# First loads, casts and V products of a fused attention and FFN kernel in another order

## The chip, the cores and the metric

The kernel runs on one core of a Trainium2 chip. The metric is the device time of one execution in microseconds. The kernel before took 264.7 us (median of three runs, 263.91 to 265.38).

## The reference

Attention over 4 batches, 8 heads, 768 positions and a head dimension of 64: every query sees the first 8 keys (the global ones) and the 96 keys up to its own position, with a bias that grows with the distance, differently in each head. The result, as 3072 tokens of 512 values, goes through a gated FFN. The inputs are float32 and so is the output.

```python
def _attn_ref(q, k, v, n_global, n_local):
    scores = scale * np.matmul(q, k.transpose(0, 1, 3, 2))
    is_global = pos[None, :] < int(n_global)
    is_local = (rel >= 0) & (rel < int(n_local))
    keep = is_global | is_local
    dist = np.where(is_global & ~is_local, float(n_local), np.abs(rel))
    scores = scores - slopes[:, None, None] * dist[None, :, :]
    scores = np.where(keep, scores, -1000000000.0)
    a = np.exp(scores - np.max(scores, axis=-1, keepdims=True))
    a = a / (np.sum(a, axis=-1, keepdims=True) + 1e-09)
    return np.matmul(a, v).astype(np.float32)

def _moe_ref(x, w_gate, w_val, w_out):
    gate = np.maximum(x @ w_gate, 0.0)
    val = x @ w_val
    return (gate * val @ w_out).astype(np.float32)
```

## The kernel before

The tokens are cut into eight halves of 384 queries (two for each batch). Each half goes through attention, head pair by head pair (four pairs of two heads), and the result `xT` (features by tokens) through the FFN: `gate` and `val` for twelve blocks of 128 hidden features, then `outp`. The order of everything is written out by hand: each engine executes its instructions in the order in which the program's calls issue them (a manual schedule), and engines wait for each other through semaphores that follow from the tiles. From the second half on, the attention of a later half is woven between the matmuls of an FFN; all FFN matmuls run on TensorE, which then hardly pauses. The change is in the first half (half 0 of batch 0), ahead of the first FFN matmul.

What the first half needs, and the names:

- `kq0`: its keys and queries in float32. `load_first(h0, h1)` issues two transfers on SyncE's queue, keys and then queries of heads h0 to h1 (line 180). Heads 0 to 1, 2 to 3, and 4 to 7 are loaded by three calls. The third is made later in the program: two one-element memsets on VectorE (line 551) write into the places that its transfers fill, so that these wait for VectorE to get there.
- `v3`: V of the first half, cast to bfloat16 by the transfer, on GpSimd's queue (line 207). Behind it on that queue: the first group of gate and value weights (`load_w_group(0)`, line 153), the keys and queries of the second half (`kq1`, four transfers, line 561), further V rows (`load_v`, line 136).
- `first_cast(p, i, copy)` (line 280): the keys (i = 0) or queries (i = 1) of head pair p to bfloat16, on VectorE (`V`), ScalarE (`A`) or GpSimd (`P`).
- `first_keys(p, copy_q)`: three transposes of the keys and three of the queries on TensorE (line 271), the queries copied to `qT` by the engine given (line 288), the keys by VectorE in three copies to `kT` (lines 258 to 260). `clear_keys(p)`: two memsets on VectorE ahead of that.
- `first_scores(0, p, g)`: bias (line 318, pairs 0 and 1 only) and score matmuls (line 327), then the exponential on ScalarE (line 333), for two groups g. `first_masks` multiplies by the bias mask on VectorE for pairs 2 and 3 (line 345); `make_mask(h)` builds a mask on ScalarE (line 238).
- `make_sel(n)` (line 235): one of three selection matrices, on VectorE. `first_values(j, copy)`: three matmuls with these bring the rows of `v3` into the order of the keys (line 303, here called the V products), and one copy by VectorE or ScalarE puts them into `vbuf` (line 305). `spread_v_globals(0, 4, NT)`: three small transfers on SyncE's queue that copy the global rows of V to later tiles (line 132).
- `first_av(0, p)`: denominators and numerators of a pair (line 448). `first_norm(0, p)`: Ln and Exp on ScalarE (lines 458 and 460) and the product `xT` on VectorE (line 463).

PSUM is given out in turn from two pools here: four tiles `t_ps` and two tiles `s_ps`.

Of the kernel before, what the change touches and what calls it, by code (L numbers as in the profile page):

```python
# [15 lines left out]
def kernel(  # L16
# [12 lines left out]
    nc = tc.nc  # L29

    B, H, S, D = q.shape
# [8 lines left out]
    NN = 3  # L40
# [4 lines left out]
    NT = -(-S // KT)  # L45
# [46 lines left out]
    vbuf = [const.tile([128, NT, (2 * H + 1) * D], BF16, name=f"vbuf{i}") for i in range(2)]  # L92
# [29 lines left out]
    def v_dst(b, r0, r1, j):  # L122
        t = vbuf[b % 2][r0:r1, j, D:]
        return t.rearrange("p (h z) -> p h z", z=2 * D)[:, :, 0:D]
# [5 lines left out]
    def spread_v_globals(b, j0=1, j1=NT):  # L130
        for j in range(j0, j1):
            nc.sync.dma_start(out=v_dst(b, 0, NG, j), in_=v_dst(b, 0, NG, 0))
# [22 lines left out]
    def load_w_group(i):  # L155
        load_w(wg[i], moe_w_gate, i * GW * 128, (i + 1) * GW * 128)
        load_w(wv[i], moe_w_val, i * GW * 128, (i + 1) * GW * 128)
# [13 lines left out]
    kq0 = firstp.tile([128, 2, H, NN * D], FP32, name="kq0")  # L171
# [6 lines left out]
    def load_first(h0, h1):  # L178
        for i, src in enumerate((k, q)):
            nc.sync.dma_start(out=kq0[:, i, h0:h1, :], in_=rows_of(src, 0, h0, h1))  # L180

    load_first(0, 2)
    load_first(2, 4)
    nc.scalar.preload_act_table_set("natural_log_exp_and_others")

    zeros = firstp.tile([128, 512], BF16)
# [43 lines left out]
    def clear_keys(p):  # L230
        nc.vector.memset(kT[0][p][:, 3, 32:128].bitcast(mybir.dt.uint32), 0)
        nc.vector.memset(kT[0][p][:, 6, NG + 48 : 128].bitcast(mybir.dt.uint32), 0)

    def make_sel(n):
        nc.vector.tensor_scalar(sel[:, n], sidx, float(n), None, op0=ALU.is_equal)
# [41 lines left out]
    def first_cast(p, i, copy):  # L277
        if p not in cast_of:
            cast_of[p] = cast_pool.tile([128, 2, NN, 2, D], BF16, name="qk")
        copy(cast_of[p][:, i].rearrange("t n e d -> t e n d"),  # L280
             kq0[:, i, 2 * p : 2 * p + 2, :].rearrange("t e (n d) -> t e n d", n=NN))

    def first_keys(p, copy_q):
        tp = psum["t"].tile([128, 512], FP32, name="t_ps")
        tp = tp[:, 0:QH].bitcast(BF16).rearrange("d (i t) -> d i t", i=2)
        for i in range(2):
            transposes(tp[:, i], cast_of[p][:, i], cast_n)
        copy_q(qTb[0][:, p, 0, :], tp[:, 1])
        put_keys(nc.vector.tensor_copy, nc.vector.tensor_copy, kT[0][p], tp[:, 0], 0)
# [10 lines left out]
    def first_values(j, copy):  # L300
        vt = psum["t"].tile([128, 512], FP32, name="t_ps")
        for n in range(NN):
            nc.tensor.matmul(vt, lhsT=sel[:, n, j, :], rhs=v3[:, :, n * D : (n + 1) * D],
                             start=(n == 0), stop=(n == NN - 1))
        copy(v_dst(0, 0, 128, j), vt.rearrange("r (h d) -> r h d", d=D))

    def first_scores(s, p, g):
        half = s % 2
        spans_ = [by[half, j] for j in steps_of[half][g]]
        ps = psum["s"].tile([128, 2, 512], FP32, name="s_ps")  # L310
        es = ef_pool.tile([128, 2, 360], BF16, name=f"ef{g}")
        cols = sum(NN * w for _, _, w, _ in spans_)
        qd = qTb[s][:, p, 0, :].rearrange("d (n t) -> d n t", n=NN)
        biased = p < HP // 2
        for e in range(2) if biased else ():
            c = 0
            for i, (j, a, w, m) in enumerate(spans_):
                nc.tensor.matmul(ps[:, e, c : c + NN * w].rearrange("k (n t) -> k n t", n=NN),
                                 lhsT=diag[:, 2 * p + e],
                                 rhs=dd[:, 0 if j == 0 else 1, :, m : m + w],  # L320
                                 start=(i == 0), stop=False, skip_group_check=True)
                c += NN * w
        c = 0
        for i, (j, a, w, m) in enumerate(spans_):
            for e in range(2):
                r = slice(64 * e, 64 * e + 64)
                nc.tensor.matmul(ps[:, e, c : c + NN * w].rearrange("k (n t) -> k n t", n=NN),  # L327
                                 lhsT=kT[0][p][r, j, :], rhs=qd[r, :, a : a + w],
                                 start=(i == 0 and not biased), stop=(i == len(spans_) - 1),
                                 skip_group_check=True)  # L330
            es_of[s, p, j] = (es, c)
            c += NN * w
        nc.scalar.activation(es[:, :, 0:cols], ps[:, :, 0:cols], AF.Exp, bias=0.0, scale=scale)  # L333

    def first_masks(s, p, g):
        for j in steps_of[s % 2][g]:
            _, a, w, m = by[s % 2, j]
            es, c = es_of[s, p, j]
            for_all = es[:, :, c : c + NN * w]
            mk = m_all[:, 2 * p : 2 * p + 2, 0 if j == 0 else 1, :, m : m + w]  # L340
            if w == WQ:
                mk = mk.rearrange("k e n p -> k e (n p)")
            else:
                for_all = for_all.rearrange("k e (n p) -> k e n p", n=NN)
            nc.vector.tensor_mul(for_all, for_all, mk)
# [92 lines left out]
    def first_av(s, p, of="t"):  # L438
        half = s % 2
        todo = [by[half, j] for g in steps_of[half] for j in g]  # L440
        av = [psum[of].tile([128, 512], FP32, name=f"{of}_ps") for _ in range(2)]
        for what in range(2):
            av3 = av[what][:, 0:QH].rearrange("d (n p) -> d n p", n=NN)
            for i, (j, a, w, m) in enumerate(todo):
                es, c = es_of[s, p, j]
                for e in range(2):
                    z0 = D + 2 * D * (2 * p + e)
                    nc.tensor.matmul(av3[64 * e : 64 * e + 64, :, a : a + w],  # L448
                                     lhsT=ones if what == 0 else vbuf[0][:, j, z0 : z0 + D],
                                     rhs=es[:, e, c : c + NN * w].rearrange("k (n p) -> k n p", n=NN),  # L450
                                     start=(i == 0), stop=(i == len(todo) - 1),
                                     skip_group_check=True)
        av_of[s, p] = av

    def first_norm(s, p):
        av = av_of[s, p]
        ln = rc_pool.tile([128, QH], FP32, name="lnd")
        nc.scalar.activation(ln, av[0][:, 0:QH], AF.Ln, bias=0.0, scale=1.0)  # L458
        rc = rc_pool.tile([128, QH], FP32, name="rcp")
        nc.scalar.activation(rc, ln, AF.Exp, bias=0.0, scale=-1.0)  # L460
        if s not in xT_of:
            xT_of[s] = xt_pool.tile([128, N_DC, QH], BF16, name="xT")
        nc.vector.tensor_tensor(xT_of[s][:, p, :], av[1][:, 0:QH], rc, op=ALU.mult)  # L463
# [77 lines left out]
    V, A, P = nc.vector.tensor_copy, nc.scalar.copy, nc.gpsimd.tensor_copy  # L541
# [5 lines left out]
    clear_keys(0)  # L547
    first_cast(0, 0, V)
    first_cast(0, 1, V)
    for i in range(2):  # L550
        nc.vector.memset(kq0[0:1, i, 4, 0:1], 0.0)
    load_first(4, H)
    first_cast(1, 0, V)
    first_cast(1, 1, A)
    first_keys(0, A)
    clear_keys(1)
    first_keys(1, A)
    load_w_group(0)
    for h0 in (0, 4):
        for i, src in enumerate((k, q)):  # L560
            nc.gpsimd.dma_start(out=kq1[:, i, h0 : h0 + 4, :], in_=rows_of(src, 1, h0, h0 + 4))
        if h0 == 0:
            first_cast(2, 0, P)
            first_cast(2, 1, P)
            first_cast(3, 0, P)
            first_cast(3, 1, P)
            nc.gpsimd.memset(vbuf[0][:, NT - 1, :].bitcast(mybir.dt.uint32), 0)
    for j in range(4, NT):
        load_v(0, j)
    first_scores(0, 0, 0)  # L570
    for n in range(NN):
        make_sel(n)
    first_scores(0, 0, 1)
    make_mask(5)
    first_scores(0, 1, 0)
    first_scores(0, 1, 1)
    first_values(0, V)
    first_values(1, A)
    first_values(2, V)
    first_values(3, A)  # L580
    spread_v_globals(0, 4, NT)
    clear_keys(2)
    first_keys(2, V)
    clear_keys(3)
    first_av(0, 0)
    first_keys(3, V)
    make_mask(6)
    first_scores(0, 2, 0)
    first_masks(0, 2, 0)
    first_scores(0, 2, 1)  # L590
    first_masks(0, 2, 1)
    first_norm(0, 0)
    first_av(0, 1)
    make_mask(7)
    first_scores(0, 3, 0)
    first_masks(0, 3, 0)
    first_scores(0, 3, 1)
    first_masks(0, 3, 1)
    first_norm(0, 1)
    first_av(0, 2)  # L600
    first_norm(0, 2)
# [101 lines left out]
```

## Time and profile before

| | |
|---|---|
| median of the runs | 264.7 us (263.91 to 265.38) |
| the profiled execution | 265.34 us |
| its span | 263.6 us |
| TensorE (PE) busy | 245.9 us, 93% |
| ScalarE (ACT) busy | 156.3 us, 59% |
| VectorE (DVE) busy | 130.7 us, 50% |
| GpSimd (POOL) busy | 91.8 us, 35% |
| first matmul of the FFN | 26.88 us |
| mean clock granted to TensorE | 0.973 |

The profile is of one execution on the hardware. Times are microseconds from the start of the span; durations of single instructions are often given in ns. PE is TensorE's matmul side and PEld its weight loads, SP is SyncE, and an engine's name with a q is its queue of instructions or transfers. A row of the timeline gives start, duration, engine, line, operation, the tiles (out<-in), a count, and in brackets the idle time before and what ended it. In a table of windows each row gives the stretch, the busy time of each engine in it with the number of its instructions, then the granted clock of TensorE (1.00 is full speed), the share of the DMA engines' time and GB/s. The chain that ended last is followed back from the last instruction, at each step to what released it.

### The profile page before, as it was taken

What the parts mean: (1) busy time and instruction counts of PE and PEld (TensorE: products, weight loads), DVE (VectorE), ACT (ScalarE), POOL (GpSimd) and SP (SyncE); (2) the same over time, 40 slices, a digit from 0 to 9 for tenths busy, and PEclk for the clock granted to TensorE, in tenths of its full rate; (3) what the DMA queues carried; (4) which work ended last, traced back from release to release, by engine and by line L of the source; (5) the groups of instructions that cost most, each with busy time, mean ns of one, the idle gap of its engine ahead of it and who ended that gap; (6) DMA issues with size and microseconds to landing.
All of it is one profiled execution on the core that took longest, in us unless ns stands there. A gap on an engine that the chain in (4) does not pass through costs nothing.

```text
span 263.6 us, 4843 instructions
## 1 busy us (share of the span) xinstructions
PE 245.9 (93%) x1716; PEld 143.4 (54%) x1725; DVE 130.7 (50%) x342; ACT 156.3 (59%) x310; POOL 91.8 (35%) x229
## 2 busy tenths in 40 slices
PE   7827898899999999999999999999999999999993
PEld 3416465466555556655665466655665566556541
DVE  5516344556444446761766257635674366714410
ACT  3617348553367577865777477756875677653311
POOL 8136639306791924550253605800540000000000
PEclk9976599999999999999999999999999999999999
DMA  6999699994895898692944995865571200021012
GB/s 144 189 187 108 80 202 124 173 272 94 148 275 141 196 204 224 113 94 94 267 93 91 102 290 110 132 75 169 173 149 52 80 0 4 0 80 42 0 40 80
DMA packets 79903, 33.54 MB, mean 127 GB/s; under 512 B 57864, under 2 KB 76808, under 8 KB 79880
## 3 DMA queue, kind: packets, MB, share of 16 engines
q1 hardware_dynamic: 48392, 24.56, 36.0%
q0 software_dynamic: 31488, 8.68, 32.1%
q8 instruction: 13, 0.21, 0.3%
q14 instruction: 10, 0.08, 0.1%
HBM read 28.36 MB, written 6.29 MB: 131 GB/s over the span
## 4 chain that ended last, share of the span: by engine, by line
PE 80%; ACT 6%; DVE 5%; DMA 5%; issue 1%; POOL 1%; SPq 0%; POOLq 0%; ACTq 0%; DVEq 0%
PE ff_ps L504 23%; PE ff_ps L485 22%; PE ff_ps L495 22%; DMA kq<-in_q_dram 5%; PE av_ps L418 5%; PE qk_ps L390 4%; DVE xT L435 2%; ACT ef L333 2%; DVE ht L497 1%; PE t_ps L271 1%; PE s_ps L327 1%; ACT grelu L488 1%; ACT lnd L458 1%; ACT rcp L432 1%; PE t_ps L448 1%
## 5 line engine op out<-in xcount | busy, mean ns | idle before, releaser
L485 PE MATMUL ff_ps<-xT,wg 128*128 128x384 bf16 x384 | 79.3, 329 | 1.5 <-DVE xT L463 0.7
L495 PE MATMUL ff_ps<-xT,wv 128*128 128x384 bf16 x384 | 78.7, 328 | 0.9 <-DVE ht L497 0.7
L488 ACT ACTIVATE grelu<-ff_ps 128x384 bf16<-128x384 f32 x96 | 47.0, 490 | 38.9 <-DVE ht L497 18.6
L497 DVE TENSOR_TENSOR ht<-ff_ps,grelu 128x384 bf16<-128x384 f32 x96 | 53.2, 555 | 29.9 <-PE ff_ps L495 23.5
L504 PE MATMUL ff_ps<-wo_sb,ht 128*128 128x512 bf16 x279 | 66.3, 378 | 0.5
L485 PEld LDWEIGHTS <-wg 128*128 128x128 bf16 x384 | 36.3, 98 | 24.9 <-issue 2.1
L495 PEld LDWEIGHTS <-wv 128*128 128x128 bf16 x384 | 36.2, 98 | 24.8 <-issue 3.6
L435 DVE TENSOR_TENSOR xT<-av_ps,rcp 64x384 bf16<-64x384 f32 x48 | 26.7, 555 | 46.1 <-ACT rcp L432 41.7
L393 ACT ACTIVATE es<-qk_ps 128x432 bf16<-128x432 f32 (+2 forms) x72 | 37.8, 529 | 10.9 <-PE qk_ps L390 9.2
L402 DVE TENSOR_TENSOR es<-es,m_all 128x432 bf16<-128x432 bf16 (+5 forms) x108 | 32.5, 330 | 23.5 <-ACT es L393 23.0
L504 PEld LDWEIGHTS <-ht 128*128 128x128 bf16 x288 | 26.9, 97 | 27.8
L348 POOL CAST kc<-ks 128x384 bf16<-128x384 f32 x24 | 11.7, 531 | 56.1 <-DMA ks<-in_k_dram 56.1
L427 ACT ACTIVATE lnd<-av_ps 64x384 f32<-64x384 f32 x48 | 23.3, 485 | 11.0 <-PE av_ps L418 10.4
L509 ACT COPY osb<-ff_ps 128x512 f32<-128x512 f32 x24 | 14.1, 586 | 24.4 <-PE ff_ps L504 23.5
L390 PE MATMUL qk_ps<-qT,kT 128*128 128x432 bf16 (+5 forms) x108 | 24.7, 286 | 0.1
L136 POOL DMA_DIRECT2D vbuf<-in_v_dram x25 | 21.5, 868 | 4.3 <-ACT lnd L458 3.8
L418 PEld LDWEIGHTS <-vbuf 128*128 128x128 bf16 x216 | 18.1, 98 | 8.2 <-issue 0.7
L418 PE MATMUL av_ps<-es,vbuf 128*128 128x216 bf16 (+4 forms) x216 | 21.1, 226 | 0.5 <-DVE xT L435 0.5
L333 ACT ACTIVATE ef<-s_ps 128x720 bf16<-128x720 f32 (+2 forms) x16 | 10.9, 707 | 12.0 <-PE s_ps L327 11.9
L356 POOL CAST qz<-qs 128x192 bf16<-128x192 f32 x48 | 14.3, 349 | 3.7 <-DMA qs<-in_q_dram 3.7
L390 PEld LDWEIGHTS <-kT 128*128 128x128 bf16 x108 | 10.6, 98 | 8.1 <-POOL vbuf L141 0.4
L432 ACT ACTIVATE rcp<-lnd 128x384 f32<-128x384 f32 x24 | 12.5, 522 | 0.8
(80 smaller groups left out, 141.7 us busy)
## 6 DMA issues: line engine op xcount, KB each, us to landing
out_dram<-osb SPq DMA_DIRECT2D x24, 256.0 KB
ks<-in_k_dram SPq DMA_DIRECT2D x6, 768.0 KB
qs<-in_q_dram SPq DMA_DIRECT2D x6, 768.0 KB
vbuf<-in_v_dram POOLq DMA_DIRECT2D x20, 120.0 KB, 4.5
wg<-in_moe_w_gate_dram POOLq DMA_DIRECT2D x3, 512.0 KB, 9.3
wv<-in_moe_w_val_dram POOLq DMA_DIRECT2D x3, 512.0 KB, 12.5
wo_sb<-in_moe_w_out_dram POOLq DMA_DIRECT2D x1, 1536.0 KB, 14.7
kq<-in_k_dram SPq DMA_DIRECT2D x2, 192.0 KB
```

What stands on the lines that cost most here:

```text
L136: nc.gpsimd.dma_start(out=v_dst(b, NG + r0, NG + r0 + n, j), in_=v[b, :, KT * j + r0 : KT * j + r0 + n, :].rearrange("h p d -> p h d"))
L390: nc.tensor.matmul(ps[:, c : c + n_], lhsT=kt[:, j, :], rhs=qd[:, :, :, a : a + w], start=True, stop=True)
L393: nc.scalar.activation(es[:, 0:cols], ps[:, 0:cols], AF.Exp, bias=0.0, scale=scale)
L402: nc.vector.tensor_mul(e4, e4, mk)
L418: nc.tensor.matmul(av3[:, :, a : a + w], lhsT=vb[:, j, z0 : z0 + 128], rhs=es[:, c : c + NN * w].rearrange("k (n p) -> k n p", n=NN), star ...
L427: nc.scalar.activation(ln[o0 : o0 + 64], av[d0 : d0 + 64, 0:QH], AF.Ln, bias=0.0, scale=1.0)
L435: nc.vector.tensor_tensor(xT_of[s][r, p, :], av_of[s, p, e_][r, 0:QH], rc[r], op=ALU.mult)
L485: nc.tensor.matmul(psg[:, 0:QH], lhsT=w_of(wg, dc, fc), rhs=xT[:, dc, :], start=(dc == 0), stop=(dc == N_DC - 1))
L488: nc.scalar.activation(gr, psg[:, 0:QH], AF.Relu, bias=0.0, scale=1.0)
L495: nc.tensor.matmul(psv[:, 0:QH], lhsT=w_of(wv, dc, fc), rhs=xT[:, dc, :], start=(dc == 0), stop=(dc == N_DC - 1))
L497: nc.vector.tensor_tensor(ht[:, fc, :], psv[:, 0:QH], st["gr"], op=ALU.mult)
L504: nc.tensor.matmul(ps2, lhsT=ht[:, fc, n * 128 : (n + 1) * 128], rhs=wo_sb[:, fc, :], start=(fc == 0), stop=(fc == N_FC - 1))
```

## The change

`load_first(4, H)` is called right behind the other two, so the memsets of line 551 go. The casts of pair 2 go to VectorE, those of pair 3 stay on GpSimd and stand ahead of the four `kq1` transfers there. The selection matrices are made behind the keys of pair 2; the V products of j = 0 and 1 stand behind these, those of j = 2 and 3 between the scores of pair 2. The query copy of pair 2 goes from VectorE to ScalarE. `spread_v_globals` and the first `first_av` and `first_norm` come later in the order. No work is added but for that, and the data moved are the same. In the changed kernel every line behind the new call has a number one higher than before (line 281 for line 280), up to the edited list itself.

```diff
     load_first(0, 2)
     load_first(2, 4)
+    load_first(4, H)
...
     clear_keys(0)
     first_cast(0, 0, V)
     first_cast(0, 1, V)
-    for i in range(2):
-        nc.vector.memset(kq0[0:1, i, 4, 0:1], 0.0)
-    load_first(4, H)
     first_cast(1, 0, V)
     first_cast(1, 1, A)
     first_keys(0, A)
     clear_keys(1)
     first_keys(1, A)
     load_w_group(0)
+    first_cast(3, 0, P)
+    first_cast(3, 1, P)
     for h0 in (0, 4):
         for i, src in enumerate((k, q)):
             nc.gpsimd.dma_start(out=kq1[:, i, h0 : h0 + 4, :], in_=rows_of(src, 1, h0, h0 + 4))
-        if h0 == 0:
-            first_cast(2, 0, P)
-            first_cast(2, 1, P)
-            first_cast(3, 0, P)
-            first_cast(3, 1, P)
-            nc.gpsimd.memset(vbuf[0][:, NT - 1, :].bitcast(mybir.dt.uint32), 0)
+    nc.gpsimd.memset(vbuf[0][:, NT - 1, :].bitcast(mybir.dt.uint32), 0)
     for j in range(4, NT):
         load_v(0, j)
     first_scores(0, 0, 0)
-    for n in range(NN):
-        make_sel(n)
+    first_cast(2, 0, V)
+    first_cast(2, 1, V)
+    clear_keys(2)
     first_scores(0, 0, 1)
     make_mask(5)
     first_scores(0, 1, 0)
+    first_keys(2, A)
+    for n in range(NN):
+        make_sel(n)
     first_scores(0, 1, 1)
     first_values(0, V)
     first_values(1, A)
-    first_values(2, V)
-    first_values(3, A)
-    spread_v_globals(0, 4, NT)
-    clear_keys(2)
-    first_keys(2, V)
     clear_keys(3)
-    first_av(0, 0)
     first_keys(3, V)
     make_mask(6)
     first_scores(0, 2, 0)
+    first_values(2, V)
     first_masks(0, 2, 0)
+    first_values(3, A)
     first_scores(0, 2, 1)
     first_masks(0, 2, 1)
-    first_norm(0, 0)
-    first_av(0, 1)
+    spread_v_globals(0, 4, NT)
+    first_av(0, 0)
     make_mask(7)
     first_scores(0, 3, 0)
+    first_norm(0, 0)
     first_masks(0, 3, 0)
     first_scores(0, 3, 1)
     first_masks(0, 3, 1)
+    first_av(0, 1)
     first_norm(0, 1)
     first_av(0, 2)
```

## The prediction

> **What bounds the kernel now.** The page is read first. The chain that ended last is TensorE's for four fifths, in the two matmul stages of the FFN, and one transfer stands out in it:
>
> ```profile
> PE 80%; ACT 6%; DVE 5%; DMA 5%; issue 1%; POOL 1%; SPq 0%; POOLq 0%; ACTq 0%; DVEq 0%
> ```
>
> The chain of waits in order of time, between 3 and 30 us, says where that transfer lies (start, us, what):
>
> ```profile
> 5.17 12.66 DMA kq<-in_q_dram
> 17.94 0.52 POOL qk L280
> 19.01 1.17 PE t_ps L448 x11
> ...
> 21.39 1.23 ACT ef L333 x2
> ...
> 27.97 0.57 DVE xT L463
> ```
>
> So from 5.17 to 17.83 us everything waits for the queries of heads 4 to 7. Then come the casts on GpSimd, and from 21.39 to 27.93 us ScalarE without a gap (exponentials, masks 6 and 7, four pairs of Ln and Exp). The last xT ends at 28.53, and from there on TensorE hardly stops: it is busy for 138.81 of the 143 us after 120 us. A microsecond won or lost ahead of 28.53 should therefore reach the end undiminished. The edits are all ahead of that point.
>
> In the transfer's shadow the timeline shows work that is done for nothing:
>
> ```profile
> 8.78 0.76 DVE L235 TENSOR_SCALAR sel<-sidx 128x512 bf16<-128x512 f32 x2
> 10.27 2.76 PE L303 MATMUL t_ps<-v,sel 128*128 128x512 bf16 x12
> 13.07 0.59 ACT L305 CAST vbuf<-t_ps 128x512 bf16<-128x512 f32 x1 [0.71 <-PE t_ps L303]
> 15.54 0.34 PE L271 MATMUL t_ps<-ident,qk 128*128 128x128 bf16 x3 [2.51 <-POOL qk L280]
> 18.51 0.50 PE L271 MATMUL t_ps<-ident,qk 128*128 128x128 bf16 x3 [2.63 <-POOL qk L280]
> ```
>
> The selection matrices, all twelve V products and their copies are over at 13.66, and TensorE then stands still but for three transposes until 18.51. The DMA queues, first in the window from 6 to 9 us and then in that from 10 to 15, show why the transfer takes 12.66 us (q1 is SyncE's queue, q0 GpSimd's; the first number is packets):
>
> ```profile
> q0 software_dynamic: 846, 0.36, 111.6%
> q1 hardware_dynamic: 7, 0.01, 0.7%
> ...
> q0 software_dynamic: 666, 0.67, 78.2%
> q1 hardware_dynamic: 658, 0.49, 39.5%
> ```
>
> The late keys and queries are issued at 4.75 and 5.17 (they wait for the memsets of line 551), but up to 9 us only V moves. After that they share packet by packet with the first weights, 658 to 666 in 5 us, 132 pairs per us. Last, the granted clock (start:end, us, then the engines' busy times with PE first, PEclk as the third value from the end):
>
> ```profile
> 14.09:17.51 3.42, 0.34 (x3) 0.17 (x3) 0.00 (x0) 0.03 (x1) 0.50 (x1) 0.93 1.29 227
> 17.51:20.92 3.41, 2.41 (x27) 1.86 (x29) 1.11 (x6) 0.00 (x0) 2.98 (x6) 0.50 0.63 76
> 24.33:27.75 3.42, 1.76 (x27) 1.24 (x25) 2.11 (x6) 3.33 (x8) 0.24 (x1) 0.93 1.28 82
> 27.75:31.16 3.41, 2.96 (x19) 1.29 (x19) 1.12 (x3) 0.67 (x2) 3.41 (x5) 0.50 0.70 52
> ```
>
> After the stretch in which TensorE worked 0.34 of 3.42 us the clock is at half, and again after one with 1.76 of 3.42.
>
> **The change, part by part.** *Issue.* The two transfers of 384 KB follow the first four on SyncE; these are issued about 0.51 us apart (0.75 to 2.28), so the new ones at 2.8 and 3.3, 2 us earlier, and the memsets go (0.07 us, in an idle gap). What counts is when packets start. After the first issue at 0.75 they start at about 2 (13 GB/s in the second from 1 to 2 us, 254 in the next); after the one at 4.75 behind 9. Issued at 2.8, while GpSimd's queue is still empty (21 packets before 5 us), they should be in the queue when the first four end, at 6.15 by the cast on ScalarE that waits for them. V needs its 1024 packets too, about 890 of them after 6.15. The rate of a V packet paired with a late one is not in the trace. Bounds: 1003 q1 packets in the 3 us from 2 to 5 and 846 q0 packets in those from 6 to 9, one after the other, give 153 pairs per us; the pair with weight packets, which are more than twice as large, runs at 132, so the same overlap could give some 215. I take 190, since both windows hold ramps. Keys: 512 / 190 = 2.7 us, landing at 8.9. Queries: 890 pairs in 4.7 us, the other 134 beside weights at 132 in 1.0, landing at 11.8 instead of 17.83. Bounds from the rates: 11.0 (V at 215) and 13.0 (153). With a lag of 4.2 us behind the issue (4.75 to 9) they start at 7.0 and end at 13.1.
>
> [...]
>
> *Casts.* Pair 2 goes to VectorE (0.44 us each by the three rows there, 0.50 on GpSimd), pair 3 stays on GpSimd but runs beside it: the second pair's casts no longer queue behind the first. But VectorE now waits in line for the queries, and behind that wait stand clear_keys(2), the keys of pair 2, the three selections and, through them, all V products. TensorE waits with the transposes ahead of scores (0,1,1). On GpSimd the casts of pair 3 now stand ahead of all four kq1 transfers and three V loads: the first two kq1 issues slide from 5.81 to about 12.3, the last two come earlier (19.79 to 14). Second-half transposes first read kq1 at 30.26 and loads land within 4.0 to 13.4 us; cost nothing, with some 5 us of cover on my timeline. spread_v_globals moves behind the first V copy; its rows are read in the second half, at 42 us, so nothing.
>
> *The new path* from the landing at 11.8: cast 0.44, three transposes and their drain 0.55 (18.51 to 19.05), the query copy on ScalarE 0.51 with the key copies behind it (at 7.07 they waited for it) 0.75: 14.05. Selections 0.36 for the first, 1.09 for all three: the first product can start at 14.45 and its group ends at 15.4 (third selection at 15.14). Then, up to the last group: three groups of V products, six transposes of pair 3, scores (0,2,0). At full clock 3 x 0.69 (2.76 for four) + 0.45 + 0.35 = 2.9; at half, with the products doubled and the longer rows for the rest, 3 x 1.38 + 0.85 + 0.6 = 5.6, and 0.4 more for the first group. The last product ends at 18.3 or 21.4; drain and ScalarE's copy 0.8; then ScalarE's row as before, 6.54 less the exponential of (0,2,0) 0.75, and the product xT 0.6: 6.4. End at 25.5 at full clock, 28.6 at half, against 28.53: a gain of 3.0 or none. Thus the 6.0 us by which the queries come earlier are mostly paid back: the selections and products (1.1 and 2.8 to 5.5 us) leave the shadow of the wait. make_mask(6) moves along with them, within ScalarE's waits.
>
> *The clock.* From 10.1 to 14.4 TensorE does six transposes and one scores piece, about 30% of the stretch. By the rows 10% brought half clock one window later and 52% did as well, while 69% (2.35 of 3.41, from 10.68) didn't. So a slow stretch is likely from 14 or 17 us, for one or two windows of 3.4 us, and hits about half of the new path: 1.5 of gain. The second slow stretch of before (27.75 to 34.57, 6.4 us of work at half clock) follows a ScalarE-bound tail; with the tail earlier and V products ahead of it, it may go, worth about 3 us, or come again. I count a fifth, 0.6.
>
> [...]
>
> Sum: 1.5 + 0.6 = 2.1 us. The profiled execution took 265.34 us (span 263.6), 0.64 above the median; it becomes 263.2, the median 264.7 becomes 262.6.
>
> **The rivals.** *Full gain:* the late loads, being first in the queue, hold V back and land at 10.5, and the clock stays up: 1.3 + 3.0 = 4.3, 260.4. For it: V's packets need to start beside a full queue. Against: the alternation 658 to 666. *The lag stays:* packets 4.2 us after the issue; landing at 13.1 costs 1.3 of the 2.1: 263.9, no change that can be told. For it: the empty q1 from 6 to 9 us; against: in that time GpSimd's queue was full, at 2.8 it isn't. *Slower:* the V products behind the queries become the bound. At mixed clock the break-even landing is 11.8 + 2.1 = 13.9, at half clock throughout 12.4. With the old landing of the keys, 14.98, as that of the queries, each us costs one: 1.1 us, and at half clock throughout 2.6; 265.8 to 267.3, say 266.3. Against it: by 17.83 both first weights had landed too (0.52 MB each in SBUF), and they now come behind in the queue of GpSimd while SyncE's is served from the start.
>
> **How the numbers follow.** About 0.5% (1.3 us) is what a measurement here can tell from no change. Forecast 0.50, with landings from 11 to 12.6 and gains of 1 to 3; full gain 0.18; lag 0.17; slower 0.15. Faster by over 1.3 us: nearly all of the forecast and the full gain, 0.65; within: 0.19; slower: 0.16, with a little of the lag. The likeliest time is 262.6. The range goes from 259.8, a little beyond the full gain, to 265.8, the near end of the slower case.
>
> **What would show it.** In the changed profile VectorE's second cast of pair 2 should start near 11.8, the first V product near 14.5, ScalarE's last Exp of the first half should end near 26.5, and xT of pair 3 near 27. The clock row should have a half stretch behind 14 us. Wrong is the prediction if the queries land before 10.5 or after 13.5, if V products still run ahead of them, or if the gain at the last xT isn't found at the end.

## The result and the profile after

The changed kernel takes 263.29 us (median of 15 runs, 261.58 to 264.45) against 265.39 for the kernel before in the same comparison (263.91 to 267.08). The ratio is 0.9918 with a 95% interval of 0.9892 to 0.9944: 0.8% faster, by 2.1 us. The profiled execution took 263.73 us with a span of 262.0, where before had 265.34 and 263.6.

The chain of waits in order of time, changed kernel, from 3 to 28 us (start, us, what):

```profile
3.31 9.43 DMA kq<-in_q_dram
12.76 0.37 DVE qk L281
...
13.56 0.49 ACT qT L289
...
14.92 0.28 DVE sel L236
...
15.24 2.74 PE t_ps L304 x6
...
19.04 2.25 PE t_ps L304 x6
...
21.31 0.58 ACT vbuf L306
...
26.65 0.48 ACT lnd L459
```

The queries land at 12.74 instead of 17.83 us, the keys ahead of them at 10.26. But the selections and both groups of V products, which before were over at 13, now lie on the chain behind them. The last xT (start, duration, from the timeline of VectorE) ends at 28.27, only 0.26 us earlier than before:

```profile
27.71 0.56 DVE L464 TENSOR_TENSOR xT<-t_ps,rcp 128x384 bf16<-128x384 f32 x1 [0.38 <-PE ff_ps L486]
```

The DMA queues from 5 to 7 and from 6 to 9 us (q0 is GpSimd's, q1 SyncE's; the first number is packets). Before, GpSimd's queue had the engines nearly alone between 6 and 9 (846 packets beside 7):

```profile
q1 hardware_dynamic: 523, 0.39, 66.3%
q0 software_dynamic: 74, 0.03, 12.5%
...
q0 software_dynamic: 571, 0.22, 61.1%
q1 hardware_dynamic: 622, 0.46, 57.3%
```

The late loads follow the first ones without a gap (244 packets of SyncE's queue from 5 to 6 us, 279 from 6 to 7), and it is V that starts later. From then on the two share the engines, one for one only from 9 to 10 us (210 and 209 packets). Behind 10 us SyncE's queue has 136 packets left, and these come slowly: 93, 36 and 7 in the next three microseconds, beside 264, 221 and 220 of GpSimd's.

The windows between changes of the clock (start:end, us, busy times of PE, PEld, DVE, ACT and POOL, then PEclk, DMA share, GB/s):

```profile
10.46:13.87 3.41, 1.22 (x18) 0.69 (x14) 0.64 (x4) 1.19 (x3) 1.62 (x3) 1.00 1.27 210
13.87:17.28 3.41, 2.12 (x9) 0.64 (x6) 2.51 (x7) 0.70 (x2) 3.41 (x6) 0.50 1.30 183
17.28:20.70 3.42, 3.42 (x17) 1.47 (x16) 1.50 (x8) 1.82 (x3) 2.24 (x3) 0.50 1.50 169
24.11:27.52 3.41, 2.33 (x35) 1.50 (x32) 2.51 (x7) 3.32 (x8) 0.26 (x1) 1.00 0.02 3
27.52:30.94 3.42, 2.81 (x35) 1.47 (x34) 1.65 (x4) 1.04 (x3) 3.42 (x5) 1.00 0.75 54
```

The clock is at half from 13.87 to 20.70, under most of the V products. It then stays full, where before fell to half a second time. (The windows of before that are shown ahead have edges 0.46 us behind the changes, hence the PEclk of 0.93; by the changes themselves, before is at half from 17.05 to 23.88 and from 27.29 to 34.12.) That is the larger part of the lead in these two profiles. The same gate matmul, that of the seventh block, which waits 0.72 us for VectorE's `ht`, starts at 50.63 before and at 48.42 here: 2.21 us earlier, of which 1.95 came after the last xT. A second wait, further on, takes some of it back (timeline of TensorE):

```profile
48.42 0.81 PE L486 MATMUL ff_ps<-xT,wg 128*128 128x384 bf16 x4 [0.72 <-DVE ht L498]
...
70.54 0.34 PE L391 MATMUL qk_ps<-qT,kT 128*128 128x432 bf16 x1 [0.51 <-DMA qT<-qz]
```

Nothing of this kind stands in the profile of before, and at the end of the span the lead is 1.6 us.

### The profile page after: what moved, and what is told of

It reads as the page before. It is cut to its first block, busy times and chain, and to the rows that moved or that the text cites. A ratio compares the mean times of both kernels' runs of the same rounds, so it can differ in the third digit from the quotient of the medians.

```text
span 262.0 us, 4848 instructions
## 1 busy us (share of the span) xinstructions
PE 246.2 (94%) x1725; PEld 141.9 (54%) x1725; DVE 129.8 (50%) x341; ACT 157.0 (60%) x311; POOL 91.1 (35%) x227
## 4 chain that ended last, share of the span: by engine, by line
PE 72%; DMA 10%; ACT 5%; DVE 4%; SPq 4%; POOL 2%; issue 1%; ACTq 0%; POOLq 0%
PE ff_ps L505 24%; PE ff_ps L496 18%; PE ff_ps L486 17%; PE av_ps L419 5%; DMA ks<-in_k_dram 5%; PE qk_ps L391 4%; DMA kq<-in_q_dram 4%; DVE xT L436 2%; PE t_ps L304 2%; SPq L360 2%; ACT ef L334 2%; DMA qT<-qz 1%; DVE ht L498 1%; SPq L364 1%; PE s_ps L328 1%
## 5 line engine op out<-in xcount | busy, mean ns | idle before, releaser
L486 PE MATMUL ff_ps<-xT,wg 128*128 128x384 bf16 x384 | 78.4, 326 | 1.6 <-DVE xT L464 0.9
L505 PE MATMUL ff_ps<-wo_sb,ht 128*128 128x512 bf16 x288 | 67.1, 378 | 0.0
L403 DVE TENSOR_TENSOR es<-es,m_all 128x432 bf16<-128x432 bf16 (+5 forms) x108 | 31.2, 318 | 24.0 <-ACT es L394 23.5
```

The source lines that it names most:

```text
L403: nc.vector.tensor_mul(e4, e4, mk)
L486: nc.tensor.matmul(psg[:, 0:QH], lhsT=w_of(wg, dc, fc), rhs=xT[:, dc, :], start=(dc == 0), stop=(dc == N_DC - 1))
L505: nc.tensor.matmul(ps2, lhsT=ht[:, fc, n * 128 : (n + 1) * 128], rhs=wo_sb[:, fc, :], start=(fc == 0), stop=(fc == N_FC - 1))
```

## The experiments

All were compared with the kernel before, which ran beside them on the same chip (medians 265.4 to 265.6). The last two columns are of one profiled execution each, in us.

| kernel | median us | ratio to before, 95% interval | queries cast | last xT ends |
|---|---|---|---|---|
| changed | 263.29 | 0.9918 (0.9892 to 0.9944) | 12.76 | 28.27 |
| e1_issue_only | 261.76 | 0.9875 (0.9822 to 0.9927) | 11.95 | 24.96 |
| e2_order_only | 268.22 | 1.0108 (1.0058 to 1.0158) | 17.86 | 32.56 |
| e3_sel_early | 260.68 | 0.9818 (0.9771 to 0.9865) | 12.03 | 25.25 |
| e4_fill | 261.65 | 0.9854 (0.9813 to 0.9895) | 12.61 | 27.70 |
| e5_before_tail_fill | 264.98 | 0.9986 (0.9958 to 1.0014) | 17.61 | 29.85 |
| e6_weights_late | 260.63 | 0.9838 (0.9795 to 0.9882) | 11.21 | 22.80 |
| e7_product_ahead | 261.60 | 0.9857 (0.9820 to 0.9893) | 13.17 | 25.08 |
| e8_issue_tail_fill | 261.75 | 0.9855 (0.9816 to 0.9894) | 12.48 | 26.54 |
| e9_sel_third_loads | 261.10 | 0.9851 (0.9805 to 0.9897) | 13.24 | 27.09 |
| e10_weights_third_loads | 259.59 | 0.9785 (0.9746 to 0.9824) | 12.59 | 26.62 |
| e11_after_third_loads | 262.27 | 0.9899 (0.9862 to 0.9936) | 12.29 | 27.67 |

**The early issue alone.** The kernel before with one edit.

```diff
     load_first(2, 4)
+    load_first(4, H)
...
-    for i in range(2):
-        nc.vector.memset(kq0[0:1, i, 4, 0:1], 0.0)
-    load_first(4, H)
```

> The kernel before with one edit: load_first(4, H) right behind the first two calls, the two memsets gone; casts and V products stay as they were. If the early issue is what pays, the queries land near 12.8 us as in the changed kernel, V is held back to about 12.5, its products run at 12.6 to 15.5 while GpSimd casts, pair 2's transposes come at about 15.6 instead of 18.5, and the time falls by about 2.5 us against before, as much as or more than the whole change gives (2.1). Rival, the new order is what pays: without it the gain is under 0.5 us, because the casts of pair 3 queue behind pair 2's on GpSimd.

It is 1.25% faster than before, 3.3 us, with a wide interval (1.9 to 4.7 us). The timelines of TensorE and GpSimd:

```profile
11.36 4.65 PE L304 MATMUL t_ps<-v,sel 128*128 128x512 bf16 x12
15.85 0.50 PE L272 MATMUL t_ps<-ident,qk 128*128 128x128 bf16 x6
...
11.95 1.41 POOL L281 CAST qk<-kq 128x384 bf16<-128x384 f32 x3 [2.76 <-DMA kq<-in_q_dram]
```

The queries are there at 11.95, and what now holds pair 2's transposes until 15.85 is TensorE with the V products, in their old place, at half clock (4.65 us for the twelve, 2.76 before). V had landed by 11.36, a microsecond earlier than expected. So the issue carries the gain; the casts on GpSimd, all done at 13.36, hide behind the products. By the medians the whole change is even 1.5 us slower than this one edit (263.29 and 261.76), with overlapping intervals: that the new order adds anything is not shown.

**The new order alone.** The changed kernel with the late issue of before.

```diff
     load_first(2, 4)
-    load_first(4, H)
...
     first_cast(0, 1, V)
+    for i in range(2):
+        nc.vector.memset(kq0[0:1, i, 4, 0:1], 0.0)
+    load_first(4, H)
```

> The changed kernel with the late issue of before put back (both memsets and the call behind the first two casts); only the new order is left. If the V products now stand behind the queries in line, nothing of them is hidden any more: the queries land near 17.5 instead of 12.74 and all behind them shifts by some 4 to 5 us, so slower than the changed kernel by 4 to 5 us and slower than before by 2 to 3. Rival, the order is good or neutral by itself: within 0.5 us of before.

1.1% slower than before, 2.9 us. VectorE's timeline shows the queries' cast and, behind it, the selections that were made at 8.45 before:

```profile
17.86 0.36 DVE L280 CAST qk<-kq 128x384 bf16<-128x384 f32 x1 [1.97 <-DMA kq<-in_q_dram]
19.99 1.34 DVE L235 TENSOR_SCALAR sel<-sidx 128x512 bf16<-128x512 f32 x3
```

This is the prediction's slower rival, in a kernel made for it: with queries at 17.8 the products behind them cost 2.9 us. At the last xT its profile is 4.03 us behind before (32.56); 1.96 of that come back up to the gate matmul of the seventh block, as this profile has no half clock there (20.14 us instead of 22.10).

**Selections early.** The changed kernel with `make_sel` ahead of pair 2's casts.

```diff
     first_scores(0, 0, 0)
+    for n in range(NN):
+        make_sel(n)
     first_cast(2, 0, V)
...
     first_keys(2, A)
-    for n in range(NN):
-        make_sel(n)
```

> The changed kernel with the three selection matrices made ahead of pair 2's casts, in VectorE's idle time from 8.85 to 10.28 us. If they are on the path as the prediction has it, the first V product starts at about 14.0 instead of 15.24 and the end comes 1.0 to 1.3 us earlier than the changed kernel's. Rival: the chain behind is set by ScalarE and the clock, the 1.2 us are given back by the tail, and the time stays within 0.4 us of the changed kernel.

0.9818 against 0.9918, and the intervals don't meet: the place of the three selections in VectorE's line costs the changed kernel time that can be told. TensorE's and VectorE's timelines:

```profile
13.60 2.66 PE L304 MATMUL t_ps<-v,sel 128*128 128x512 bf16 x6
16.79 1.47 PE L304 MATMUL t_ps<-v,sel 128*128 128x512 bf16 x6
...
8.95 1.39 DVE L236 TENSOR_SCALAR sel<-sidx 128x512 bf16<-128x512 f32 x3
```

The first product starts 1.57 us behind the queries' cast instead of 2.48: 0.9 us for the selections, near the forecast. The medians differ by 2.6 us, more than that. In this profile the queries landed 0.7 us earlier and the second six products ran at full clock (1.47 us instead of 2.30). How much of the rest is due to the edit and how much to where the clock's windows fell isn't settled.

**Zeros where TensorE stood idle.** Twelve matmuls whose result nobody reads.

```diff
+    fill_pe(7)
     first_keys(2, A)
...
     first_scores(0, 1, 1)
+    fill_pe(5)
     first_values(0, V)
```

> The changed kernel with twelve more matmuls on zeros, whose result nobody reads: seven ahead of pair 2's transposes and five ahead of the first V product, where TensorE stood idle from 10.9 to 15.2 us. If TensorE's emptiness there is what brings the half clock from 14.3 to 21.2 us, the clock stays full there, six V products take about 1.4 instead of 2.74 us, the last xT ends 1.5 to 2.5 us earlier than 28.27 and the time falls by as much. Rival: the clock falls anyway, a little later, in the tail that waits for ScalarE, or the zeros delay the transposes; then no gain or a loss of up to 1 us.

0.9854, 1.6 us below the changed kernel by the medians; the intervals just meet. In the profile the clock didn't stay up: it was at half from 7.29, before the zeros, so that they ran at half and held pair 2's transposes to 14.14. But it came back at 14.12, and the products show it:

```profile
17.34 1.36 PE L304 MATMUL t_ps<-v,sel 128*128 128x512 bf16 x5 [0.38 <-DVE sel L236]
19.24 1.47 PE L304 MATMUL t_ps<-v,sel 128*128 128x512 bf16 x6
```

Six products in 1.47 us against 2.74 and 2.30 in the changed kernel. That the zeros did this isn't shown by the one profile, as the clock fell ahead of them. Over all runs the mean granted clock is 0.993 in the six with zeros and 0.981 in the fifteen of the changed kernel, so work that is of no use does seem to shorten the time at half clock.

**Zeros in the tail of before, and of the early issue.** Six matmuls each, to keep the second half-clock stretch away.

```diff
     first_norm(0, 1)
+    fill_s(2)
     first_av(0, 2)
+    fill_s(2)
     first_norm(0, 2)
     first_av(0, 3)
+    fill_s(2)
     first_norm(0, 3)
```

> The kernel before with six matmuls on zeros, read by nobody, in three places of the tail of its first half (behind first_norm(0, 1), first_av(0, 2) and first_av(0, 3)), where TensorE waits for ScalarE between 24.6 and 28.5 us. If the second half-clock stretch of before (27.75 to 34.57) comes from that emptiness, it is gone, the FFN and transposes behind 28.5 run at full clock, and the time falls by about 2 us: what the changed kernel won at its end beyond its 0.26 us at the last xT. Rival: the clock falls all the same or the zeros delay the tail; within 0.6 us of before.

> The kernel before with the early issue only, and six matmuls on zeros in the tail as above. Its profile had half clock from 22.53 to 29.36 us; if the zeros keep it up, 1.5 to 2 us faster than with the early issue only, near 260. Rival: no difference, then the clock of that stretch hides behind ScalarE and the DMA.

Neither expectation held, but their rivals did: no difference from before (0.9986), none from the early issue alone (261.75 against 261.76). TensorE's timeline of the first of the two:

```profile
24.39 1.01 PE L544 MATMUL s_ps<-zeros 128*128 128x512 bf16 x2 [1.38 <-ACT ef L333]
26.50 1.03 PE L544 MATMUL s_ps<-zeros 128*128 128x512 bf16 x2
```

The zeros need an `s_ps` tile and wait 1.38 us for ScalarE, and `first_av(0, 2)` waits behind them; the last xT ends 1.32 us later than before. Its queries came 0.3 us earlier, but the first half-clock stretch ran on to 28.09 instead of 23.88, which also slows this tail (eight matmuls take 0.71 us at 25.32, where before has 0.45 at 25.56). Yet the clock is full from there, and from the last xT to the gate matmul with the 0.72 us wait it takes 20.37 us (29.85 to 50.22) instead of 22.10. The changed kernel, without zeros, takes 20.15. The other profiles agree on this distance: 20.14 to 20.16 us in the seven without zeros in the tail whose clock is full behind the last xT, 21.42 to 22.10 in the three with a half-clock stretch that lasts 3.9 us or more beyond it (before, e1 and e9). So the second stretch is worth 1.3 to 2.0 us; this way of removing it costs as much.

**First weights behind the casts.** On the kernel with the selections early.

```diff
-    load_w_group(0)
     first_cast(3, 0, P)
     first_cast(3, 1, P)
+    load_w_group(0)
```

> The kernel with the selections early (changed kernel plus that edit) and the first weight group issued behind the casts of pair 3 on GpSimd instead of ahead of them. If the last queries are slowed by the weight packets that they share the engines with, the queries land 0.7 to 1 us earlier, near 11.3, and so does the last xT: 0.5 to 1 us faster than the kernel with the selections early. Rival: the weights, 1 MB issued at about 12 and 13 us ahead of kq1 and V rows, land too late for the FFN near 24 us or push kq1 behind 27; slower by 1 us or more.

The median is the same as with the selections early (260.63 and 260.68). In the profile the queries land at 11.19 and the last xT ends at 22.80, 2.45 us earlier; but in the later kernel with the weights late (e10) the queries were cast at 12.59. Over these profiles the cast starts between 11.21 and 13.24 us, so whether the weight packets delay the queries stays open. They aren't needed for a late landing: in e10 the first weights are issued at 13.26 us, only 83 packets of SyncE's queue and 181 of GpSimd's are left at 10 us, and the queries still land at 12.57. Much of the rest of the 2.45 us is the clock, which stays full under all V products here (the first six take 1.47 us instead of 2.66). What the profile does show is where an early lead goes. At the gate matmul it leads before by 7.06 us (43.57), at the end by 5.6:

```profile
66.64 0.34 PE L391 MATMUL qk_ps<-qT,kT 128*128 128x432 bf16 x1 [1.46 <-POOL vbuf L141]
```

This is the same matmul as that at 70.54 in the changed kernel, the first scores of the third half. Though the row names GpSimd, it starts in both profiles 2.05 to 2.07 us behind the end of the issue of the third half's last query transpose (64.59 and 68.47).

**One V product ahead of the transposes.** Also on the kernel with the selections early.

```diff
+    first_values(0, V)
     first_keys(2, A)
     first_scores(0, 1, 1)
-    first_values(0, V)
     first_values(1, A)
```

> The kernel with the selections early, and the first V product (j = 0) ahead of pair 2's transposes, where TensorE waits for the queries from 11.2 to 12.45 us. With V landed by 11.4 (the products of the kernel with only the early issue started at 11.36) one group of products goes into the shadow again: 0.4 to 1 us faster than the kernel with the selections early. Rival: at half clock the group takes 1.3 us and delays the transposes; no difference within 0.4 us.

No gain (0.9857 against 0.9818, overlapping). TensorE's timeline:

```profile
12.20 1.44 PE L304 MATMUL t_ps<-v,sel 128*128 128x512 bf16 x3 [1.70 <-DMA v<-in_v_dram]
13.44 0.85 PE L272 MATMUL t_ps<-ident,qk 128*128 128x128 bf16 x6
```

V itself lands at 12.2 here and the queries at 13.2. One group does fit between the two, and from the queries' cast to the last xT it takes 11.91 us instead of 13.22 with the selections early. But the queries came 1.1 us later than there, which took that back, and in the medians no gain shows. The shadow that is left lasts only from V's landing to the queries'.

**The third half's loads earlier.** On three kernels: with the selections early, with the first weights late as well, and on the changed kernel itself.

```diff
-    for f in (F[0], F[1], K[0], ...
+    for f in (lambda: load_qk_after(2), F[0], F[1], K[0], ...
...
-              lambda: load_qk_after(2), AV[2], F[8], ...
+              AV[2], F[8], ...
```

> The kernel with the selections early, and load_qk_after(2), the third half's keys and queries, called ahead of the first FFN matmul instead of behind F[7], so some 17 us earlier. If part of the early gain is given back because the third half's queries come late out of their transfer and transposes, this has cover now; the lag of 0.1 to 0.3 us near 66 us is gone, little is won: 0 to 0.5 us faster than with the selections early. Rival: the loads share the engines with the second weight groups, these come late for F[8], and the time grows by 0.5 us or more.

> The kernel with the selections early and the first weights late, and the third half's loads ahead of the first FFN matmul. There 1.46 us of TensorE's time went to a wait near 66.6 us for what comes out of the third half's loads. If that is the next bound it goes, and this is 1 to 1.4 us faster than without the earlier loads, near 259.4. Rival: the second weight groups come late; slower by 0.5 us or more.

> The changed kernel itself with the third half's loads ahead of the first FFN matmul. In its profile the lead over before falls from 2.21 us at 47 us to 1.8 behind the wait of 0.51 us at 70.54 for the third half's queries. If the late loads are the cause, that wait is gone, the lead is kept to the end, and the time falls by about 0.5 us, to 262.8. Rival: no change, because the DMA engines are full there in any order, or a loss through late weights.

The wait of the third half's first scores is in none of the three profiles. On the changed kernel the lead over before at the end of the FFN's matmuls is no longer smaller than at 47 us but larger (2.8 becomes 3.1); with the weights late it goes from 3.85 to 4.15, where without these loads 7.06 had become 5.5. In the medians the step isn't resolved: 262.27 against 263.29 for the changed kernel and 259.59 against 260.63, both with overlapping intervals, and 261.10 against 260.68 with the selections alone, whose lag there was small. The wait is also absent without these loads with the selections early, in e4 and in e7, which led before by 5.2, 2.8 and 5.4 us at the gate matmul; so it doesn't come in every execution, and that the earlier loads remove it rests on one profile each. Its price in the time is between nothing and a microsecond or so. The kernel with all three edits has the lowest median, 0.9785 of before (0.9746 to 0.9824), and beats the changed kernel's 0.9918; from the selections alone (0.9818) it can't be told.

## Why the prediction was right, and where not

Forecast was 262.6 from 264.7, a gain of 2.1 us, and 2.1 us were measured (263.29 from 265.39). The sign and its cause, the early issue, hold. That the sum met the measurement is in good part luck: several terms were off, in opposite directions. One of the prediction's own signs of being wrong is near: "the gain at the last xT isn't found at the end". In the profiles 0.26 us were won there and 1.6 at the end, most of it somewhere else.

*Issue and landing.* That the late loads would join the queue behind the first four without the lag of 4.2 us was right, and the rival of the lag is out, as is the full gain's landing at 10.5 (the earliest of any profile is 11.19): 523 packets of SyncE's queue between 5 and 7 us, 1456 by then, where the first four loads, each half the size of the keys' 512, have 1024. The rate, taken as 190 pairs per us, was right on average too (571 and 622 packets in the three microseconds from 6). The landing came 0.9 us late, at 12.74 for 11.8, within the bounds of 11.0 to 13.0; the keys came 1.4 us late, at 10.26 for 8.9. The 523 packets in 2 us are 262 per us, though V had hardly begun; the window from 2 to 5 had promised 334. And the tail was mis-sized: for the last 134 packets the sum had 1.0 us, while the 136 that were left at 10 us took 2.7. A rate of pairs doesn't describe them, as e10 shows, where the tail is as slow with nearly empty queues. (The first packets, taken to start at about 2, move at 1.87, 1.1 us behind the start of the first issue and 0.7 behind its end.)

*The path behind it.* From the landing to the first product 2.65 us were forecast (11.8 to 14.45) and 2.50 measured (12.74 to 15.24). From the end of the last product to the last xT, 7.2 forecast, 7.0 measured (21.27 to 28.27). That the selections are on this path is confirmed by e3_sel_early, where the same distance shrank by 0.9 us. That the V products leave the shadow is confirmed by e2_order_only. What the prediction didn't see is that with early queries the shadow is gone whatever the order: in e1_issue_only the products still stand first and TensorE works on them until 15.85, four microseconds behind the queries' landing.

*The clock, first stretch.* Half of the new path was put at half clock. From the first product to the end of the last the sum had 3.85 us at full and 6.95 at half clock; 6.03 were measured, so it was some 0.7 of the way, as the clock was at half from 13.87 to 20.70. The last xT came at 28.27 where the sum had 27.0, 0.26 us of gain for the 1.5: 0.9 of the difference is the landing, some 0.6 the clock, and the shorter steps ahead of the first product and behind the last gave a little back.

*The clock, second stretch.* A chance of a fifth was put on its going away, 0.6 us of about 3 (6.4 us of work at half clock; 6.1 by the clock's own edges). It went, and gave 1.95 (22.10 to 20.15 us between the last xT and the gate matmul); e5_before_tail_fill, another kernel without it, shows 1.7. A likely reason, not tested, is the work in the window ahead: 2.33 us from 24.11 where before had 1.80 from 23.88. Both readings are of one execution each, and the windows fall differently from run to run: the two profiles have mean clocks of 0.973 and 0.987, but the 39 runs of before beside the experiments have 0.975 on average and the 15 of the changed kernel 0.981. One of the 15 had a mean clock of 1.0 and took 263.70 us all the same. So over the 15 runs the sum came out as forecast, but the split of these profiles isn't the usual one, and the clock's usual share stays open.

*"Should reach the end undiminished."* Not quite. The lead of 2.21 us fell to 1.6, for here the third half's queries don't move up by as much as TensorE does (1.79 us). They became the next bound at 70.54; the wait is larger in e6_weights_late and absent in e11_after_third_loads, but absent in some profiles without that edit too.

*What went with half clock.* The half-clock stretches here are all multiples of 3.41 us: one in e6_weights_late (3.41), two in the changed kernel and, twice, in before (6.83), three in e5_before_tail_fill (10.24). Taken between the changes of the clock, the windows ahead of a half-clock stretch had up to 2.06 us of work (1.22 in the changed kernel, 0.34 and 1.80 in before). The prediction's 69% (2.35 us) was read from a window taken 0.46 us late; from 10.22 it had 2.81 us. In the first 40 us, full windows not followed by half clock had 2.12 us or more in twelve of the thirteen profiles. The thirteenth, e5_before_tail_fill, has two with 1.91 and 1.75, so the work in the window alone doesn't tell what follows. Rows of TensorE's windows (third value PEclk here) from the kernels with the weights late, with the selections early (two) and with zeros in the tail of before:

```profile
17.48:20.89 3.41, 2.04 (x42) 1.00 1.42 200
...
5.81:9.22 3.41, 1.89 (x23) 1.00 1.27 233
19.46:22.87 3.41, 2.12 (x42) 1.00 1.68 123
...
11.02:14.44 3.42, 1.75 (x9) 1.00 1.18 232
```

Behind the first two the clock falls to half, at 20.89 and 9.22; behind the other two it doesn't.

## What to carry to other kernels

Ask first what sits in the shadow of the wait that you shorten: here 5.1 us of earlier landing brought 2.1, because products that were free became the path, and the cheapest remedy was to move three small instructions out of the line behind the remaining wait, into idle time ahead of it. Measure such an edit alone as well: the early issue without the new order did no worse. Read the granted clock window by window as part of that path, in windows whose edges lie where it changes: here a stretch of 3.41 us in which TensorE worked 2.06 us or less was mostly followed by half clock, and six products then took 2.74 us instead of 1.47. And when an early stage gets faster, look at the next loads that are issued relative to it, for they may not follow.

## What was not expected of the hardware

With the late loads in SyncE's queue (523 packets between 5 and 7 us, 68 before), V's packets from GpSimd's queue began at about 7 us rather than at 5, though they were issued at 2.56 in both kernels: 74 of them between 5 and 7 us, against 550 in the same two microseconds before. The same two loads, issued at 2.79 and 3.31 in every kernel with the early issue, were ready for their last cast anywhere from 11.21 to 13.24 us. And a busy TensorE did not always bring the full clock back at once: with the early issue alone it was busy for 3.38 of the 3.41 us from 8.42, and the clock stayed at half through the next window too, to 15.24, while with the weights late one window with 3.03 us of work, from 20.89, was enough.
